# Re-ordering loads, weights and layer norm in a fused attention and MLP kernel

## The chip, the cores and the metric

The kernel runs on one core of one Trainium2 chip. TensorE (PE, with its weight loads as PEld), VectorE (DVE), ScalarE (ACT), GpSimd (POOL) and SyncE (SP, which here only issues DMAs) each work through their own queue in order. The metric is the device time of one execution in microseconds; lower is better.

## The reference

Causal attention with a position bias for 8 batches of 8 heads, 576 tokens and 64 dimensions, then a layer norm and a two-layer MLP on the heads put side by side, with a residual.

```python
scores = (1 / sqrt(64)) * q @ k.T
cum = cumsum(maximum(s, 0), axis=-1)
bias = -(cum[:, :, :, None] - cum[:, :, None, :])
scores = where(causal, -1e9, scores + minimum(bias, 0))
attn = softmax(scores)                      # 8 x 8 x 576 x 576
x = heads side by side of (attn @ v)        # 8 x 576 x 512
xn = (x - mean(x)) / sqrt(var(x) + 1e-6) * g_ln
out = x + maximum(xn @ w_ch1, 0) @ w_ch2    # 512 -> 2048 -> 512
```

## The kernel before

The order is written out by hand. The main loop has 64 **slots**, n = 0 to 63, one for each head h of each batch b. The 576 tokens are four blocks of 128 and a rest of 64.

A slot does, in this order: `scores(b, h)` (five matmuls into three PSUM tiles sa, sb, sc; one exponential on ACT for each; four triangular masks on POOL); in even slots `scores_d`, the 64 x 64 rest blocks of two heads (tile sd); two units of MLP work; `pv` of the head before (15 matmuls into the single tile pot, and then on DVE a reciprocal and two scaled copies, called the evacuation below); two more units. The softmax sum comes out of a column of ones in v.

The scores need q and k with the head dimension on partitions (qT, kT), with four more rows that carry the bias as bf16 parts of the cumulative sum; `aug` writes these by small DMAs. Each qT or kT buffer holds four heads, and there are two of each. `qk_pair` makes the 64 main rows for two heads: 10 TensorE transposes into two PSUM tiles (tag tr), four DVE copies out of them. It stands in even slots, at their start, for the two heads that begin two slots later. The tag tr has two buffers, which trqk (qk_pair), sd (scores_d) and trx (layer norm) share.

Loads for the next batch go out on SP's queue, two tiles of 256 KB in a slot, and POOL turns them to bf16 one slot later. q, k and v all lie in DRAM as (head, token, 64), and each tile takes 128 tokens of 8 heads, so that every piece is one token of one head, 256 bytes. q is scaled by 1/8 in its cast.

**Weights.** In the eight slots of batch 0, `w1_part` and `w2_part` load and cast two parts of the weights at the start of each slot: 16 parts of 512 KB through two staging buffers. The w1 cast, with the layer-norm gain folded in, is DVE's, and the w2 cast POOL's.

**Layer norm.** `ln_stats` takes statistics in two parts, after pv of heads 5 and 7; `ln_aggr` adds them up, with a power on POOL for the inverse root. At the end of slot h = 1 of the next batch `ln_tile` follows for all four tiles of the batch (five in odd batches, where the fifth, xm, holds the 64-token rests of two batches): xn on DVE, four transposes on PE, a copy on DVE, tile by tile.

**MLP units.** Then 32 units are queued: 16 `mlp1` (four matmuls into a ph tile and a relu, every fourth on DVE and the others on ACT) and 16 `mlp2` (a quarter of a py tile each; after the last quarter DVE adds the residual and SP sends the rows). ph and py share two buffers. Four units run in a slot, so the units of batch 0 begin in slot 10. After slot 63 follow the last units of batch 6, the layer norm of batch 7, and 64 units: batch 7 and the rest rows of all batches.

Of the kernel before, what the change touches and what calls it, by code (L numbers as in the profile page):

```python
# [12 lines left out]
ALU = mybir.AluOpType  # L13
# [6 lines left out]
def kernel(  # L20
# [33 lines left out]
    xnp = ctx.enter_context(tc.tile_pool(name="xnp", bufs=3))  # L54
# [16 lines left out]
    q_bf = [const.tile([P, NT, H, D], BF16, name=f"q_bf{i}") for i in range(2)]  # L71
    k_bf = [const.tile([P, NT, H, D], BF16, name=f"k_bf{i}") for i in range(2)]
# [17 lines left out]
    nc.sync.dma_start(out=c_in, in_=s_flat)  # L90


    def load(src, b, t, h0, h1, eng):
        pn = P if t < NF else TL
        tmp = stage.tile([P, h1 - h0, D], F32, name="qkvtmp", tag="st")
        eng.dma_start(
            out=tmp[:pn],
            in_=src[b, h0:h1, t * P : t * P + pn, :].rearrange("h s d -> s h d"),
        )
        return tmp, pn  # L100

    def cast(kind, b, t, h0, h1, tmp, pn, eng):
        if kind == "v":
            dst = v_bf[b % 2][:pn, t, h0:h1, 0:D]
        else:
            dst = (q_bf if kind == "q" else k_bf)[b % 2][:pn, t, h0:h1, :]
        if eng == "act":
            nc.scalar.activation(
                out=dst, in_=tmp[:pn], func=ACT.Copy, scale=scale if kind == "q" else 1.0
            )  # L110
        elif eng == "dve":
            if kind == "q":
                nc.vector.tensor_scalar_mul(out=dst, in0=tmp[:pn], scalar1=scale)
# [12 lines left out]

    first = [(n, t, 0, 4) for t in range(NT) for n in ("k", "q")]
    first_tmp = []
    for i, (n, t, h0, h1) in enumerate(first[:6]):
        first_tmp.append(load(SRC[n], 0, t, h0, h1, nc.sync))  # L130

    make_identity(nc, ident)
    nc.vector.memset(c_one, 1.0)
    nc.vector.memset(mhalf, -0.5)
    for i in range(2):
        nc.gpsimd.memset(q_bf[i][TL:P, NF, :, :], 0.0)
        nc.gpsimd.memset(k_bf[i][TL:P, NF, :, :], 0.0)
# [16 lines left out]
    nc.vector.tensor_copy(out=c_mid, in_=c_in)
    nc.vector.tensor_tensor(out=c_in, in0=c_in, in1=c_mid, op=ALU.subtract)
    nc.vector.tensor_copy(out=c_lo, in_=c_in)

    def aug(b, g):
        r0 = b * H + g * G
        i = (b * 2 + g) % 2  # L160
        for j, src in ((1, c_hi), (2, c_mid), (3, c_lo)):
            nc.sync.dma_start(out=kT[i][D + j : D + j + 1, :, 0:S], in_=src[r0 : r0 + G, :])
        nc.sync.dma_start(out=qT[i][D : D + 1, :, 0:S], in_=c_neg[r0 : r0 + G, :])


    def qk_pair(b, j):
        g, i = j // 2, (b * 2 + j // 2) % 2
        hh = (j % 2) * 2
        for src, dst in ((k_bf, kT), (q_bf, qT)):
            tr = ps_t.tile([P, SP], BF16, name="trqk", tag="tr")  # L170
# [353 lines left out]
```

## Time and profile before

| | us |
|---|---|
| median of 3 runs | 502.89 |
| the runs | 500.87 to 503.55 |
| the profiled execution, its own time | 504.88 |
| its span, first to last instruction | 503.2 |
| TensorE busy | 397.9 (79%) |
| DVE, ACT, POOL busy | 245.9, 174.1, 174.9 |

Shares over the whole span mix a stretch that waits for loads (up to about 94 us), one in which attention and MLP are interleaved (94 to 442 us), and a tail of MLP units alone. The page's 40 slices and its chain of waits tell these apart.

### The profile page before, as it was taken

The page shows a single profiled execution, that of the slowest core. Times are in us where ns is not written, and L with a number is a line of the kernel's source. Part 1 is how long each engine was busy: PE and PEld are TensorE (multiplying, and loading weights), DVE is VectorE, ACT ScalarE, POOL GpSimd, SP SyncE. Part 2 cuts the span into 40 slices and gives each one's busy share as a digit, 9 for nine tenths or more (in the row PEclk, how much of TensorE's full clock was granted, in tenths as well). Part 3 has the DMA queues.
Part 4 walks back from the last instruction along what each step waited for, and adds up shares of the span by engine and source line. Part 5 has one row for each costly group of instructions (what it writes and reads, how often), then busy time and mean ns, then how long its engine had stood idle before and what let it go on. Part 6 is the DMA issues. An engine that isn't in the chain of part 4 may idle for free.

```text
span 503.2 us, 8135 instructions
## 1 busy us (share of the span) xinstructions
PE 397.9 (79%) x2960; PEld 212.6 (42%) x2960; DVE 245.9 (49%) x614; ACT 174.1 (35%) x343; POOL 174.9 (35%) x439
## 2 busy tenths in 40 slices
PE   0303655899779987998699969986999799699996
PEld 0102434455345544554355535543554455344442
DVE  8324545447644554466445554665455445612111
ACT  2022422373226422642165226422642264041220
POOL 9324487253514442444334424442343122000000
PEclk9998555699959995999599979997999799999999
DMA  5499899141554056406640574066401000100103
GB/s 101 103 219 271 228 280 221 18 86 32 150 104 87 24 136 126 86 7 150 129 85 3 149 136 86 11 150 126 86 21 57 22 1 22 42 21 30 55 8 76
DMA packets 122487, 47.10 MB, mean 94 GB/s; under 512 B 114448, under 2 KB 114704, under 8 KB 122448
## 3 DMA queue, kind: packets, MB, share of 16 engines
q1 hardware_dynamic: 122448, 46.60, 40.4%
q8 instruction: 23, 0.38, 0.3%
q14 instruction: 16, 0.13, 0.1%
HBM read 36.85 MB, written 9.44 MB: 92 GB/s over the span
## 4 chain that ended last, share of the span: by engine, by line
PE 69%; DVE 14%; DMA 8%; POOL 5%; issue 1%; SPq 1%; POOLq 0%
PE ph L339 27%; PE py L357 25%; PE pot L260 5%; DMA w1tmp<-in_moe_w_ch_dram 4%; PE trx L329 4%; DVE xn L319 3%; DMA w2tmp<-in_moe_w_ch_dram 3%; DVE xT L334 2%; DVE kT L178 2%; PE sb L189 2%; PE sc L189 2%; PE sa L189 2%; DVE yo L366 2%; DVE hT L347 2%; PE trqk L172 2%; DVE kT L177 2%
## 5 line engine op out<-in xcount | busy, mean ns | idle before, releaser
L357 PE MATMUL py<-w_bf,hT 128*128 128x512 bf16 x576 | 135.2, 383 | 0.0
L209 POOL TENSOR_SCALAR_AFFINE_SELECT e<-e 128x128 bf16<-128x128 bf16 x256 | 71.7, 295 | 169.1 <-ACT e L199 150.6
L339 PE MATMUL ph<-xT,w_bf 128*128 128x512 bf16 x512 | 129.3, 400 | 0.0
L199 ACT ACTIVATE e<-sa 128x512 bf16<-128x512 f32 x64 | 38.2, 597 | 189.8 <-PE sa L189 183.2
L349 ACT ACTIVATE hT<-ph 128x512 bf16<-128x512 f32 x108 | 64.8, 600 | 80.4 <-PE ph L339 79.8
L339 PEld LDWEIGHTS <-w_bf 128*128 128x128 bf16 x576 | 55.2, 101 | 62.4 <-issue 13.3
L357 PEld LDWEIGHTS <-hT 128*128 128x128 bf16 x576 | 53.6, 98 | 56.8 <-issue 1.6
L268 DVE RECIPROCAL rinv<-pot 128x5 f32<-128x5 f32 x64 | 12.5, 195 | 110.5 <-PE pot L260 110.4
L260 PEld LDWEIGHTS <-e 128*128 128x128 bf16 x960 | 41.5, 103 | 23.4 <-POOL e L209 8.3
L260 PE MATMUL pot<-v_bf,e 128*128 128x65 bf16 x960 | 44.5, 202 | 7.0 <-POOL e L209 7.0
L329 PE MATMUL trx<-ident,xn 128*128 128x128 bf16 x144 | 18.5, 269 | 37.8 <-DVE xn L319 37.8
L347 DVE TENSOR_SCALAR hT<-ph 128x512 bf16<-128x512 f32 x36 | 24.9, 692 | 46.0 <-PE ph L339 46.0
L189 PEld LDWEIGHTS <-kT 68*128 68x128 bf16 x320 | 28.8, 109 | 25.1 <-issue 8.5
L207 ACT ACTIVATE e<-sc 128x512 bf16<-128x512 f32 x64 | 38.7, 605 | 0.0
L203 ACT ACTIVATE e<-sb 128x512 bf16<-128x512 f32 x64 | 37.9, 592 | 0.0
L225 PE MATMUL sd<-qT,kT 68*128 68x64 bf16 x64 | 8.3, 216 | 35.8 <-DVE kT L178 35.8
L366 DVE TENSOR_TENSOR yo<-py,xb 128x512 f32<-128x512 f32 x32 | 22.1, 690 | 25.8 <-PE py L357 25.3
L172 PE MATMUL trqk<-ident,k_bf 128*128 128x128 bf16 x160 | 18.5, 256 | 18.9 <-POOL k_bf L123 14.1
L329 PEld LDWEIGHTS <-xn 128*128 128x128 bf16 x144 | 10.5, 115 | 47.1 <-DVE xn L319 46.9
L123 POOL CAST v_bf<-qkvtmp 128x512 bf16<-128x512 f32 (+3 forms) x39 | 22.1, 587 | 23.9 <-DMA qkvtmp<-in_v_dram 23.9
L189 PE MATMUL sc<-qT,kT 68*128 68x320 bf16 (+1 forms) x128 | 28.6, 311 | 0.0
L189 PE MATMUL sb<-qT,kT 68*128 68x64 bf16 (+1 forms) x128 | 28.6, 308 | 0.0
(60 smaller groups left out, 391.2 us busy)
## 6 DMA issues: line engine op xcount, KB each, us to landing
out_dram<-yo SPq DMA_DIRECT2D x32, 256.0 KB
qkvtmp<-in_k_dram SPq DMA_DIRECT2D x28, 256.0 KB
qkvtmp<-in_q_dram SPq DMA_DIRECT2D x28, 256.0 KB
qkvtmp<-in_v_dram SPq DMA_DIRECT2D x28, 256.0 KB
w1tmp<-in_moe_w_ch_dram SPq DMA_DIRECT2D x8, 512.0 KB
w2tmp<-in_moe_w_ch_dram SPq DMA_DIRECT2D x8, 512.0 KB
qkvtmp<-in_k_dram SPq DMA_DIRECT2D x15, 128.0 KB
qkvtmp<-in_q_dram SPq DMA_DIRECT2D x15, 128.0 KB
```

Of the source, the lines that this page charges most:

```text
L189: nc.tensor.matmul(dst, lhsT=kk[0:KA, hh, kb * P : (kb + 1) * P], rhs=qq[0:KA, hh, q0:q1], start=True, stop=True,)
L199: nc.scalar.activation(out=e[:, u, 0:512], in_=a, func=ACT.Exp)
L203: nc.scalar.activation(out=e[:, u, OB : OB + 512], in_=a, func=ACT.Exp)
L207: nc.scalar.activation(out=e[:, u, OC : OC + 512], in_=a, func=ACT.Exp)
L209: nc.gpsimd.affine_select(out=e[:, u, o : o + P], in_=e[:, u, o : o + P], compare_op=ALU.is_ge, fill=0.0, base=0, pattern=[[1, P]], channe ...
L260: nc.tensor.matmul(pot[:, t, :], lhsT=e[:, u, o : o + P], rhs=vv[:, kb, h, :], start=(kb == 0), stop=(kb == last),)
L329: nc.tensor.transpose(tr[:, kd, :], xn[:, kd * P : (kd + 1) * P], ident)
L339: nc.tensor.matmul(ph, lhsT=w1_bf[:, kd, fb * P : (fb + 1) * P], rhs=xT[:, kd, :], start=(kd == 0), stop=(kd == KD - 1),)
L347: nc.vector.tensor_scalar_max(out=hT[:, fb, :], in0=ph, scalar1=0.0)
L349: nc.scalar.activation(out=hT[:, fb, :], in_=ph, func=ACT.Relu)
L357: nc.tensor.matmul(py[0], lhsT=hT[:, fb, t * P : (t + 1) * P], rhs=w2_bf[:, fb, :], start=(fb == 0), stop=(fb == FB - 1),)
L366: nc.vector.tensor_add(out=yo, in0=py[0], in1=x)
```

## The change

- **q and k loads.** One load brings two heads of one batch: 96 partitions, six neighbouring tokens on each, so that a piece is 6 x 64 floats, 1,536 bytes. `qk_pair` then has 12 transposes of 96 columns, one for each of the six tokens, and its four copies read the PSUM tile with a step of 96 elements to put the tokens back in order. It stands in odd slots, for the two heads that begin in the next slot. v is loaded as before.
- **Scale.** The factor 1/8 moves from the q cast into the exponential; the cumulative sums are multiplied by 8.
- **Order of loads and casts.** A function `pre(n)` lists them by slot; from slot 17 on it casts one q or k tile in a slot and loads the one two pairs ahead. In batch 0 and 1 some casts go to DVE and ACT.
- **Weights.** w1 is loaded in slots 2 and 9, w2 from slot 10, through four buffers; the casts stand in slots 9 to 14.
- **Start.** The first loads are heads 0 to 3 of q and k; the first two `aug` go through ACT's queue; fills of qT, kT and v_bf change size and engine.
- **Layer norm.** `ln_xn` does all xn tiles of a batch right after its statistics (slot h = 0); `ln_tr` does transposes and copies in slots h = 1 (two tiles) and h = 2 (the others), with an MLP unit between. The units of a batch are queued after slot h = 2; those of batch 0 still begin in slot 10, with three in slots 14 to 17.
- **relu.** DVE takes the first MLP unit of each slot if it is an mlp1, instead of every fourth.

The core of the diff (`cast` and `ld` take care of names and buffers):

```diff
-    stage = ctx.enter_context(tc.tile_pool(name="stage", bufs=8))
-    wst = ctx.enter_context(tc.tile_pool(name="wst", bufs=2))
+    stage = ctx.enter_context(tc.tile_pool(name="stage", bufs=2))
+    pairs = ctx.enter_context(tc.tile_pool(name="pairs", bufs=3))
+    wst = ctx.enter_context(tc.tile_pool(name="wst", bufs=4))
...
+        nc.sync.dma_start(
+            out=tmp[0:QP],
+            in_=src[b, 2 * j : 2 * j + 2].rearrange("h (p t) d -> p h (t d)", t=QT),
+        )
...
-            for t in range(NT):
+            for t in range(QT):
                 nc.tensor.transpose(
-                    tr[:, t * P : (t + 1) * P],
-                    src[b % 2][:, t, 2 * j : 2 * j + 2, :],
-                    ident,
+                    tr[:, t * QP : (t + 1) * QP],
+                    src[0:QP, t, :, :],
+                    ident[0:QP, 0:QP],
                 )
-            nc.vector.tensor_copy(out=dst[i][0:D, hh, :], in_=tr[0:D, :])
-            nc.vector.tensor_copy(out=dst[i][0:D, hh + 1, :], in_=tr[D : 2 * D, :])
+            for u in range(2):
+                copy_on(
+                    engs[n],
+                    dst[i][0:D, hh + u, 0:S].rearrange("d (p t) -> d p t", t=QT),
+                    tr[u * D : (u + 1) * D, :].rearrange("d (t p) -> d p t", t=QT),
+                )
...
+        elif n == 9:
+            cast("v", 1, 4, "pool")
+            for i in range(4):
+                cast_w1(i)
+                ld_w1(4 + i)
...
-        if h == 1 and b > 0:
-            for t in range(len(x_tiles(b - 1))):
-                ln_tile(b - 1, t)
+        lt = {1: (0, 1), 2: (2, 3, 4)}.get(h, ()) if b > 1 else ()
+        if n == 9:
+            lt = range(NF)
+        for t in lt:
+            ln_tr(b - 1, t)
+            if n != 9 and t != 1 and t != 4:
+                run_units(1)
+                nu -= 1
+        run_units(nu - 2)
+        if n == 9 or (b > 1 and h == 2):
             queue += batch_units(b - 1)
```

**The layer norm on DVE.** Batch 2's, around slots h = 0 and 1 of batch 3. Before, xn and the copy xT alternate at the end of h = 1:

```order
L366 TENSOR_TENSOR yo_2135<-py_2097,xb_818 128x512
L319 TENSOR_SCALAR xn_2139<-xb_1454,mv_2057,rs_2058 128x512
L334 COPY xT_2138<-trx_2141 128x4x128
L319 TENSOR_SCALAR xn_2147<-xb_1454,mv_2057,rs_2058 128x512
L334 COPY xT_2138<-trx_2149 128x4x128
```

Now:

```order
L348 TENSOR_SCALAR xn_2017<-xb_1424,mv_2004,rs_2005 128x512
L404 TENSOR_TENSOR yo_2029<-py_1962,xb_754 128x512
L108 COPY kT0_106<-trqk_2038 64x576 x2
L108 COPY qT0_104<-trqk_2047 64x576 x2
L297 RECIPROCAL rinv_2097<-pot_2081 128x5
L299 TENSOR_TENSOR xb_2080<-pot_2081,rinv_2097 128x4x64
L306 TENSOR_SCALAR xm1_112<-pot_2081,rinv_2097 64x64
L369 COPY xT_2012<-trx_2101 128x4x128
L369 COPY xT_2012<-trx_2111 128x4x128
```

All xn now stand together in h = 0, ahead of qk_pair's copies; the copies xT stand behind those and behind an evacuation.

**An mlp1 slot with a qk_pair on DVE.** Before, the fourth relu of the slot ahead stands in front of the copies:

```order
L347 TENSOR_SCALAR hT_96<-ph_2316 128x512
L177 COPY kT1_108<-trqk_2328 64x640
L178 COPY kT1_108<-trqk_2328 64x640
L177 COPY qT1_106<-trqk_2336 64x640
L178 COPY qT1_106<-trqk_2336 64x640
L268 RECIPROCAL rinv_2392<-pot_2376 128x5
```

Now:

```order
L108 COPY kT1_107<-trqk_2209 64x576 x2
L108 COPY qT1_105<-trqk_2218 64x576 x2
L385 TENSOR_SCALAR hT_99<-ph_2242 128x512
L297 RECIPROCAL rinv_2270<-pot_2254 128x5
L299 TENSOR_TENSOR xb_2080<-pot_2254,rinv_2270 128x4x64
```

The relu of the slot's own first unit now follows the four copies.

**SP's queue in batch 0.** Before, weights stand between the loads of q and k from the first slot on:

```order
L413 DMA gln<-in_moe_g_ln_dram 128x4x1
L420 DMA w1tmp<-in_moe_w_ch_dram 128x1024 x2
L96 DMA qkvtmp<-in_k_dram 128x8x64
L96 DMA qkvtmp<-in_q_dram 128x8x64
L420 DMA w1tmp<-in_moe_w_ch_dram 128x1024 x2
```

Now:

```order
L90 DMA ktmp<-in_k_dram 96x2x384
L90 DMA qtmp<-in_q_dram 96x2x384
L491 DMA gln<-in_moe_g_ln_dram 128x4x1
L90 DMA ktmp<-in_k_dram 96x2x384
L90 DMA qtmp<-in_q_dram 96x2x384
L99 DMA vtmp<-in_v_dram 128x8x64 x3
L90 DMA ktmp<-in_k_dram 96x2x384
L90 DMA qtmp<-in_q_dram 96x2x384
L145 DMA w1tmp<-in_moe_w_ch_dram 128x2x512 x4
```

Half of w1 is issued in batch 0, behind nearly half of batch 1's loads, and the rest from slot 9.

## Rows read from the trace of the kernel before

**Rows 1.** The page: the span in 40 slices of 12.6 us.

```profile
PE   0303655899779987998699969986999799699996
PEclk9998555699959995999599979997999799999999
DMA  5499899141554056406640574066401000100103
GB/s 101 103 219 271 228 280 221 18 86 32 150 104 87 24 136 126 86 7 150 129 85 3 149 136 86 11 150 126 86 21 57 22 1 22 42 21 30 55 8 76
```

**Rows 2.** Start, in order of time: start, duration, engine, operation [idle before, releaser].

```profile
4.30 0.42 ACT L108 ACTIVATE k_bf<-qkvtmp 128x256 bf16<-128x256 f32 x1 [2.24 <-DMA qkvtmp<-in_k_dram]
8.11 0.42 ACT L108 ACTIVATE k_bf<-qkvtmp 128x256 bf16<-128x256 f32 x1 [1.39 <-DMA qkvtmp<-in_k_dram]
8.40 2.22 POOL L141 MEMSET qT<- 4x2560 bf16 x1
8.68 2.25 DVE L154 CAST c_mid<-c_in 64x576 bf16<-64x576 f32 x1
19.37 0.63 PE L189 MATMUL sa<-qT,kT 68*128 68x512 bf16 x1
36.65 0.75 DVE L421 TENSOR_SCALAR w_bf<-w1tmp,gln 128x1024 bf16<-128x1024 f32 x1 [0.71 <-DMA w1tmp<-in_moe_w_ch_dram]
38.48 0.29 PE L225 MATMUL sd<-qT,kT 68*128 68x64 bf16 x2 [17.61 <-DVE kT L178]
```

**Rows 3.** The chain that ended last, its landmarks: start, duration, engine and line.

```profile
94.21 3.41 PE ph L339 x8
...
397.79 3.41 PE ph L339 x8
...
428.11 5.18 PE py L357 x24
...
442.39 14.30 PE ph L339 x64
456.68 13.81 PE py L357 x64
...
498.64 0.69 DVE yo L366
```

**Rows 4.** The same chain over two slots between layer norms.

```profile
206.72 0.69 DVE hT L347
...
208.36 0.23 PE sd L225 x2
208.59 1.73 PE ph L339 x8
210.32 0.46 PE pot L260 x15
...
212.51 0.22 PE sa L189
...
217.10 0.69 DVE hT L347
```

**Rows 5.** Groups by shape: count | busy us, mean ns | idle before, releasers.

```profile
L178 DVE COPY kT<-trqk 64x640 bf16<-64x640 bf16 x32 | 15.8, 493 | 0.4
L270 DVE TENSOR_TENSOR xb<-pot,rinv 128x256 f32<-128x256 f32 x64 | 27.2, 425 | 2.2
L366 DVE TENSOR_TENSOR yo<-py,xb 128x512 f32<-128x512 f32 x32 | 22.1, 690 | 25.8 <-PE py L357 25.3 <-issue 0.3
L334 DVE COPY xT<-trx 128x512 bf16<-128x512 bf16 x32 | 13.6, 425 | 19.5 <-PE trx L329 19.5
L306 POOL TENSOR_TENSOR rs<-rs,mhalf 128x5 f32<-128x5 f32 x4 | 4.7, 1176 | 16.2 <-DVE rs L305 16.2
```

**Rows 6.** Layer norm of one batch on DVE, in order of time.

```profile
231.59 0.20 DVE L268 RECIPROCAL rinv<-pot 128x5 f32<-128x5 f32 x1 [1.50 <-PE pot L260]
232.60 0.87 DVE L295 BATCH_NORM_STATS2 stats<-xb 128x6 f32<-128x128 f32 x4
234.10 0.17 DVE L305 TENSOR_SCALAR rs<-mv 128x5 f32<-128x5 f32 x1
238.49 0.54 DVE L319 TENSOR_SCALAR xn<-xb,mv,rs 128x512 bf16<-128x512 f32 x1
```

**Rows 7.** Busy time by stretch: PE, PEld, DVE, ACT, POOL, then granted clock, DMA.

```profile
190.00:196.40 6.40, 4.42 (x30) 3.05 (x31) 4.14 (x9) 0.87 (x2) 0.20 (x1) 0.50 1.19 203
196.40:199.80 3.40, 3.40 (x12) 1.22 (x11) 0.00 (x0) 1.45 (x4) 2.31 (x7) 0.50 0.01 2
206.70:217.10 10.40, 9.94 (x88) 5.41 (x86) 5.06 (x12) 6.77 (x13) 4.77 (x13) 1.00 0.54 101
```

More of the change, by code (lines that the diff above doesn't have):

```diff
@@ L102, in cast, with copy_on @@
-    def cast(kind, b, t, h0, h1, tmp, pn, eng):
+        tmp = stage.tile([P, H, D], F32, name="vtmp", tag="vtmp", bufs=3)
+        nc.sync.dma_start(
+            out=tmp[:pn], in_=v[b, :, t * P : t * P + pn, :].rearrange("h s d -> s h d")
+        )
+        return tmp
+    def copy_on(eng, out, in_):
+        if eng == "act":
+            nc.scalar.copy(out=out, in_=in_)
+        elif eng == "dve":
+            nc.vector.tensor_copy(out=out, in_=in_)
+        else:
+            nc.gpsimd.tensor_copy(out=out, in_=in_)
@@ L154, with cast @@
[L154 to L158, printed above, removed]
+            loaded[kind, b, i] = load_qk(k if kind == "k" else q, b, i, kind + "tmp")
+    def cast(kind, b, i, eng):
+        if b >= B:
+            return
+        tmp = loaded.pop((kind, b, i))
+        if kind == "v":
+            pn = P if i < NF else TL
+            copy_on(eng, v_bf[b % 2][:pn, i, :, 0:D], tmp[:pn])
+        else:
+            t = pairs.tile([P, QT, 2, D], BF16, name=kind + "p", tag=kind + "p")
+            copy_on(
+                eng,
+                t[0:QP].rearrange("p t h d -> p h t d"),
+                tmp[0:QP].rearrange("p h (t d) -> p h t d", d=D),
+            )
+            ready[kind, b, i] = t
@@ L425, in w2_part, with run_units @@
-    def w2_part(c):
-        tmp = wst.tile([P, 2, Dm], F32, name="w2tmp", tag="w")
-        nc.sync.dma_start(out=tmp, in_=w2_r[:, 2 * c : 2 * c + 2, :])
-        nc.gpsimd.tensor_copy(out=w2_bf[:, 2 * c : 2 * c + 2, :], in_=tmp)
     queue = []
     pend = []
-    def run_units(n):
-        for _ in range(n):
+    def run_units(n, dve_first=False):
+        for i in range(n):
             if queue:
+                first_unit[0] = dve_first and i == 0
                 queue.pop(0)()
-    slots = [(b, h) for b in range(B) for h in range(H)]
@@ new lines @@
+    c_in, c_sc, c_one = c_in[0:BH], c_sc[0:BH], c_one[0:BH]
+    nc.sync.dma_start(out=c_in, in_=s.rearrange("b h s -> (b h) s"))
+    ld("k", 0, 0)
+    ld("q", 0, 0)
+    ld("k", 0, 1)
+    ld("q", 0, 1)
+    for t in range(3):
+        ld("v", 0, t)
+    make_identity(nc, ident)
+    nc.vector.memset(c_one, 1.0)
+    nc.vector.memset(ones4, 1.0)
+    for i in range(2):
+        nc.vector.memset(kT[i][0:KA, :, S:SP], 0.0)
+        nc.scalar.dma_start(out=kT[i][D + 3 : D + 4, :, 0:S], in_=ones4)
@@ new lines @@
+    nc.vector.tensor_copy(out=c_mid, in_=c_in)
+    nc.vector.tensor_tensor(out=c_lo, in0=c_in, in1=c_mid, op=ALU.subtract)
+    cast("k", 0, 1, "act")
+    qk_pair(0, 0, ("act", "act", "dve", "dve"))
+    aug(0, 0, nc.scalar)
+    nc.vector.memset(qT[1][D : D + 3, :, :], 1.0)
+    aug(0, 1, nc.scalar)
+    for i in range(2):
+        nc.gpsimd.memset(v_bf[i][:, 0:NF, :, D : D + 1], 1.0)
+        nc.gpsimd.memset(v_bf[i][TL:P, NF, :, :], 0.0)
+        nc.gpsimd.memset(v_bf[i][0:TL, NF, :, D : D + 1], 1.0)
@@ L462 @@
+    NU = {10: 4, 11: 4, 12: 4, 13: 4, 14: 3, 15: 3, 16: 3, 17: 3, 18: 4}
+    for n in range(B * H):
+        b, h = n // H, n % H
+        nu = NU.get(n, 4)
+        pre(n)
+        if h % 2 == 1 and n > 1:
+            g = (n + 1) // 2
+            qk_pair(g // 4, g % 4)
         scores(b, h)
+        if n == 0:
+            qk_pair(0, 1)
+        run_units(1, True)
         if h % 2 == 0:
             scores_d(b, h // 2)
-        run_units(2)
+        run_units(1)
         if pend:
@@ L494 @@
     queue += mixed_units()
-    run_units(len(queue))
+    while queue:
+        run_units(4, True)
 _INS = ['q', 'k', 'v', 's', 'moe_g_ln', 'moe_w_ch1', 'moe_w_ch2']
```

337 lines of the change are left out of this document (199 added, 138 removed).

## The prediction

> **What bounds the kernel now.** I read the 40 slices first, then the chain that ended last, then each stage by its own rows. The slices show three stages [rows 1]. In the first seven, to about 90 us, PE is busy 0 to 6 tenths while DMA moves over 200 GB/s in five of them. From then to slice 35 PE stands at 9 tenths, with a dip once a batch in which the granted clock drops too. The last five are MLP alone.
>
> *Start and batch 0.* The first scores run at 19.37 us and the second slot's only behind the scores_d at 38.48, after PE idled 17.6 us [rows 2]. It waited for DVE's copies into kT, and DVE for a w1 load: the cast at 36.65 stands ahead of the copies in DVE's queue. Weights gate all eight slots like this, and the first MLP unit starts at 94.21 [rows 3].
>
> *Main stage.* Six batches take 397.79 - 94.21 = 303.6 us, 50.6 each [rows 3]. Two slots between layer norms take 217.10 - 206.72 = 10.4 us [rows 4] with PE busy 9.94 at full clock [rows 7], so PE is the bound there: eight such slots would be 41.5. [...]
>
> *Tail.* From 428.11 on, six units, a layer norm, two units, and 64 units in 56 us, PE-bound [rows 3].
>
> **The change part by part.** The prices of PE work come from rows 4: a unit is 1.73 / 2 = 0.87 us; scores 3 x 0.22 = 0.65; pv 0.46; scores_d 0.12, half of its 0.23, since the next unit overlaps its tail. For the new transposes (12 of 96 columns for 10 of 128) I take 0.55 as an estimate: all of an even slot, 212.51 - 206.72 = 5.8, less the wait of the scores_d, leaves about that.
>
> *The new copies* decide most. Today 64x640 costs 0.493 and 128x512 bf16 0.425 [rows 5], 0.53 ns an element over a base of 0.155, so 576 would cost 0.46. From PSUM in float32, 256 cost 0.425 and 512 cost 0.690: 1.04 ns an element. Both are 4 bytes in 1.04 ns, and the bf16 rows get two neighbours for it. The new copies read with a step of 96 elements, so 4 bytes hold one wanted element: 0.16 + 576 x 1.04 ns = 0.76 us. I take 0.76 with 0.46 as the lower end; no row reads bf16 with a step, so the upper end is open, and the third rival prices it.
>
> [...]
>
> *Start.* The s load and four q/k loads go out first; before, six tiles of 128 KB land between the casts at 4.30 and 8.11 [rows 2], 0.2 MB a us, so the first 2.1 MB (to the third v tile) land by 12. DVE gets one more fill (2560 elements; POOL's took 2.22) ahead of the cumulative sum, whose casts take up to 2.25 each [rows 2], and has c_lo by 12. The aug DMAs follow on ACT and land at 15: first scores at 15, where 19.4 stands now. The last v tile is issued only when DVE has cast an earlier one, behind two copies and another 2.2 us fill: at 16, landing at 18.5; DVE then casts k and copies, and the second slot's scores run at 21 (now 38.6).
>
> *Slots 1 to 7.* No weight cast stands in them. DVE has, per two slots, four copies (3.04), two evacuations of 1.0 (231.59 to 232.60 [rows 6]) and a cast of some 0.6: 5.6 us, and statistics once. PE at half clock needs about as much. Since the chain copies, scores, pv, evacuation closes on itself I take 3.45 a slot: slot 8 at 45.3.
>
> *Slots 8 and 9* load DVE most. After pv at 47.6: evacuation 1.0, statistics and sums 1.5 (1.67 for five tiles, 232.60 to 234.27 [rows 6]), the power on POOL 1.1 [rows 5], four xn of 0.5 to 0.54 [rows 6], eight half-size w1 casts of 0.45 (0.75 for twice the size [rows 2]), four copies, an evacuation, four xT copies of 0.425 with their transposes. That is 63; with the scores of slot 10 at half clock the **first MLP unit starts at 64** instead of 94.2.
>
> *Weights.* What is left of w1 and w2 then, 6.3 MB, moves behind slots 9 to 14 with 0.6 MB of q and k, from 54 us to the unit that needs the last part, near 90. At the 219 to 280 GB/s of the weight slices [rows 1] that is 25 to 32 us of 36: hidden. The w2 casts, about 1 us each, fall on POOL between masks that pv needs a slot later; they too are covered.
>
> *Main slots.* An even slot is 0.65 + 0.12 + 0.46 + 4 x 0.87 = 4.7: the scores_d finds its PSUM buffer free, since the copies now end a slot earlier. An odd one is 0.55 + 0.65 + 0.46 + 3.46 = 5.1. In mlp1 slots the relu of the first unit stands behind the four copies: copies from 0.45 to 3.55 after the slot's start, relu to 4.3. The third unit wants that PSUM buffer, and PE gets to it at 3.4: it waits 0.9, twice a batch.
>
> *Layer norm.* Count from the start of slot h = 0. pv ends at 2.95; DVE then needs 1.0 + 1.67, POOL's power 1.18, five xn 2.5, a yo 0.69 [rows 5, 6], and is at 10.0. Then come the four copies of slot h = 1, and the first transposes of the layer norm need the PSUM buffer of the k copies: 11.5. PE gets there at 4.7 + 3.4 = 8.1 and waits 3.4, and 0.4 for the next. The idle can drop the clock again; as the echo cost 1.7 (half of 3.4 [rows 7]) when it came, I take 1.0.
>
> A batch: 4 x 4.7 + 2 x 5.1 + 2 x 6.0 + 4.5 x 0.22 for transposes (four of 128 columns stream what sa's 512 do) + 3.8 + 1.0 = **46.9**, against 50.6.
>
> *Sum.* First unit at 64. To the start of slot 19: 32 units 27.7, eight scores 5.2, nine pv 4.1, transposes and scores_d 3.9, mlp1 waits 1.8, a layer norm with two units fewer to cover it 5.6, cold start 1.7: 50, so 114. Five batches of 46.9: 348.5. Slots 59 to 63: 26, so 374.5. Tail: pv, 76 units 65.8, transposes 1.1, 0.5 twice for relus (14.30 against 13.81 [rows 3]), 1.5 for the layer norm among seven units: 69.9, so 444.4. Last add and store as now, 503.2 - 498.64 = 4.6: a span of 449.0. The profiled execution took 1.7 more than its span, and the median lies 2.0 below it: **449**.
>
> **The rivals.**
>
> *1. The copies keep today's rate (0.46).* Then the mlp1 waits go (14 x 0.9 = 12.6), each of six layer norms waits 1.0 less (6), and batches 0 and 1 lose some 6 of DVE work: 424. For it: today's copies are all at that rate. Against it: the 4 bytes a step above.
>
> *2. Loads hold the start after all, so that the change doesn't do what it says there.* Up to slot 10, 7.1 MB of q, k, v and 2.1 MB of w1 must come, at 165 GB/s if slot 9 is to be where I put it. Rows 1 show 101 and 103 GB/s in the first two slices, where SP's queue waited on casts, and the new order also waits for casts on three engines. At 130 GB/s the first unit would be 14 us later: 463; and should weights also come late in slots 10 to 14, up to 475. Against it: 1,536-byte pieces, and 219 to 280 GB/s once the queue is full.
>
> *3. Strided copies cost far more, and DVE is the bound: slower than before.* Without them DVE has per batch 8 evacuations, statistics, five xn and xT, four relus and four yo, 21.9 us; with 16 copies at 0.76 it is 34, below 46.9. Each 0.1 us on a copy adds 1.6. To lose all 54 us in six and a half batches, a batch must take 55: copies of 2.1 us, from where it decides. At 2.3 the batch is 58.7 and the time 526. For it: no row shows the pattern. Against it: float32 from PSUM with a step (out of pot, 65 apart) costs its plain 1.04 ns an element.
>
> **How the numbers follow.** Forecast 449 (437 to 461 by the slot rate of batch 0 and the clock after layer norms): 0.62. Rival 1, 418 to 432: 0.16. Rival 2, 455 to 478: 0.18. Rival 3, above 503: 0.03; near no change, if two of them meet: 0.01. The range 424 to 470 takes in the middle of rival 1 and most of rival 2. A measurement of this kernel can tell about 0.5% from no change; faster by more 0.96, within 0.01, slower by more 0.03.
>
> **What would show it.** Copies of 0.76 (or 0.46) in the groups by shape. First MLP unit near 64, with DVE and not DMA ahead of it in the chain. PE waits of some 0.9 for the relu's buffer in odd mlp1 slots, and of 3 to 4 in slot h = 1, with a smaller clock dip. 47 us from batch to batch. Batch 0 slots that wait for loads, or a batch of over 50 us, would prove the sum wrong.

## The result, and the profile after

The changed kernel takes 446.46 us (median of 4 runs, 445.89 to 447.1) beside 502.19 for the kernel before on the same chip: a ratio of 0.889, with a 95% interval of 0.886 to 0.892. The prediction was 449, with 424 to 470 as its range. The profiled execution took 447.1 with a span of 445.4. One of e6's four runs below fell into a slower state (448.2 us, at a granted clock of 0.928 where the others had 0.943 to 0.959) and is left out of its median.

The page of after, the 40 slices of 11.1 us, to be held against [rows 1]:

```profile
PE   1396459995999799969998899889997999999995
...
PEclk9999999997999899988999999969999999999999
DMA  7887075964531354134511551154221000101013
GB/s 198 214 231 199 10 243 174 271 197 119 143 107 55 101 149 115 29 96 129 142 56 52 162 152 54 53 149 125 71 76 47 26 1 24 72 0 72 24 26 71
```

PE stands at 9 tenths from the seventh slice on (67 us), with dips; before, from the ninth (101 us). The first two slices move 198 and 214 GB/s where they moved 101 and 103. PE's dips in the main stage are still there, once a batch, but shallower, and so are those of the clock: from 118 us on its lowest slices are at 6 and 8 tenths, where those of before stand at 5 and 7.

The landmarks of the start, from the order of time on PE (start, duration, engine, line, operation, count, and in brackets the idle time before it with its releaser):

```profile
14.57 0.59 PE L213 MATMUL sa<-qT,kT 68*128 68x512 bf16 x1 [6.91 <-DMA qT<-c_neg]
...
21.17 0.58 PE L213 MATMUL sa<-qT,kT 68*128 68x512 bf16 x1 [1.26 <-ACT e L222]
...
43.71 0.61 PE L213 MATMUL sa<-qT,kT 68*128 68x512 bf16 x1 [2.41 <-DVE qT L108]
...
58.37 0.61 PE L364 MATMUL trx<-ident,xn 128*128 128x128 bf16 x4 [7.81 <-DVE kT L108]
...
63.45 0.63 PE L377 MATMUL ph<-xT,w_bf 128*128 128x512 bf16 x1
```

Where [rows 2] have scores at 19.37 and the second slot's not before 38.48, they now start at 14.57 and 21.17, and the first MLP unit comes at 63.45. On the same view of before it comes at 94.02, so the start gave 30.6 us. The first units of later batches follow at 117.98, 163.27, 211.23, 255.31, 303.33 and 347.41: five periods of 45.9 us on average, where before has 50.3. That gave 21.9 more, and these two make up 52.4 of the 57.8 us by which the span fell; the period from the first to the second batch is 2.2 longer, and what follows the last of these units 7.6 shorter.

The copies into kT and qT, from the groups by shape (count, then busy us, mean ns, then idle before and its releaser):

```profile
L108 DVE COPY kT<-trqk 64x576 bf16<-64x576 bf16 x62 | 46.6, 751 | 8.3 <-PE trqk L191 7.5
L108 DVE COPY qT<-trqk 64x576 bf16<-64x576 bf16 x64 | 48.3, 754 | 1.4
```

They cost half as much again as the larger copies of [rows 5], as forecast.

One layer norm of five tiles, in order of time on POOL, DVE and PE:

```profile
193.04 1.17 POOL L335 TENSOR_TENSOR rs<-rs,mhalf 128x5 f32<-128x5 f32 x1 [2.95 <-DVE rs L334]
...
194.25 2.39 DVE L348 TENSOR_SCALAR xn<-xb,mv,rs 128x512 bf16<-128x512 f32 x4 [1.29 <-POOL rs L335]
...
197.74 1.51 DVE L108 COPY kT<-trqk 64x576 bf16<-64x576 bf16 x2
199.28 1.52 DVE L108 COPY qT<-trqk 64x576 bf16<-64x576 bf16 x2
199.30 0.61 PE L364 MATMUL trx<-ident,xn 128*128 128x128 bf16 x4 [3.98 <-DVE kT L108]
```

And the busy times there, as in [rows 7]: stretch, its length, PE, PEld, DVE, ACT, POOL busy, then granted clock, DMA share and GB/s:

```profile
195.20:199.30 4.10, 0.12 (x5) 0.00 (x2) 4.02 (x9) 0.00 (x0) 2.58 (x5) 0.79 0.14 51
199.30:204.80 5.50, 5.27 (x21) 2.64 (x23) 3.74 (x8) 0.53 (x2) 0.00 (x0) 0.54 0.44 114
```

DVE works without a gap from the power on POOL to the kT copies, and PE stands still beside it for 4 us; behind that the granted clock is 0.54 for 5.5 us. The layer norm is spread, but one wait in front of it is left, and it is DVE's queue that holds it.

### The profile page after: what moved, and what is told of

It reads as the page before. It is cut to its first block, busy times and chain, and to the rows that moved or that the text cites. A ratio compares the mean times of both kernels' runs of the same rounds, so it can differ in the third digit from the quotient of the medians.

```text
span 445.4 us, 8185 instructions
## 1 busy us (share of the span) xinstructions
PE 377.6 (85%) x2973; PEld 208.6 (47%) x3024; DVE 280.8 (63%) x615; ACT 174.1 (39%) x339; POOL 171.4 (38%) x415
## 4 chain that ended last, share of the span: by engine, by line
PE 65%; DVE 17%; issue 7%; POOL 5%; ACT 3%; DMA 1%; POOLq 0%; SPq 0%; ACTq 0%
PE ph L377 27%; PE py L395 21%; PE pot L289 4%; DVE xn L348 4%; DVE kT L108 4%; PE sa L213 3%; PE sb L213 3%; PE trqk L191 3%; DVE qT L108 3%; PE sc L213 2%; PE trx L364 2%; ACT hT L387 2%; POOL rs L335 2%; DVE yo L404 1%; POOL e L236 1%
## 5 line engine op out<-in xcount | busy, mean ns | idle before, releaser
L236 POOL TENSOR_SCALAR_AFFINE_SELECT e<-e 128x128 bf16<-128x128 bf16 x256 | 77.3, 315 | 169.4 <-ACT e L222 169.1
L395 PE MATMUL py<-w_bf,hT 128*128 128x512 bf16 x550 | 140.1, 392 | 1.9 <-issue 0.7
L377 PE MATMUL ph<-xT,w_bf 128*128 128x512 bf16 x489 | 121.3, 382 | 4.9 <-ACT hT L387 3.3
L395 PEld LDWEIGHTS <-hT 128*128 128x128 bf16 x576 | 54.3, 100 | 52.4 <-issue 4.6
L108 DVE COPY kT<-trqk 64x576 bf16<-64x576 bf16 x62 | 46.6, 751 | 8.3 <-PE trqk L191 7.5
L108 DVE COPY qT<-trqk 64x576 bf16<-64x576 bf16 x64 | 48.3, 754 | 1.4
L213 PEld LDWEIGHTS <-kT 68*128 68x128 bf16 x320 | 27.2, 106 | 37.3 <-issue 17.1
L364 PE MATMUL trx<-ident,xn 128*128 128x128 bf16 x144 | 16.3, 247 | 29.3 <-DVE kT L108 26.0
L213 PE MATMUL sa<-qT,kT 68*128 68x512 bf16 x64 | 27.7, 433 | 11.5 <-DMA qT<-c_neg 6.9
L299 DVE TENSOR_TENSOR xb<-pot,rinv 128x256 f32<-128x256 f32 x64 | 27.2, 425 | 2.2
L110 POOL CAST qp<-qtmp 96x768 bf16<-96x768 f32 x31 | 26.2, 846 | 4.4 <-DMA qtmp<-in_q_dram 4.4
```

The lines of the kernel that those rows point to most:

```text
L108: nc.vector.tensor_copy(out=out, in_=in_)
L110: nc.gpsimd.tensor_copy(out=out, in_=in_)
L213: nc.tensor.matmul(dst, lhsT=kk[0:KA, hh, kb * P : (kb + 1) * P], rhs=qq[0:KA, hh, q0:q1], start=True, stop=True,)
L236: nc.gpsimd.affine_select(out=e[:, u, o : o + P], in_=e[:, u, o : o + P], compare_op=ALU.is_ge, fill=0.0, base=0, pattern=[[1, P]], channe ...
L299: nc.vector.tensor_tensor(out=xb[b][:, :, hs], in0=pot[:, 0:NF, 0:D], in1=rinv[:, 0:NF].unsqueeze(2).to_broadcast([P, NF, D]), op=ALU.mult,)
L364: nc.tensor.transpose(tr[:, kd, :], xn[:, kd * P : (kd + 1) * P], ident)
```

## The experiments

My theory had four parts: the weights had held the start; the copies cost 0.75 us because of their step of 96 elements; DVE is on the path only in batches 0 and 1 and at the layer norm; what is left of the layer norm is DVE's order. The rivals: copies on the path everywhere, large load pieces as the source of the gain, and a spread layer norm that merely moved the wait.

The first units in the table are read from the order of time on PE; "per batch" is the mean of the five periods behind the second batch's first unit. In the kernel before, e4 and e5 a batch's units start in slot h = 2, in e6, e10, e11 and e13 in h = 4, in the others in h = 3, so columns two and three compare only within such a group; the periods compare everywhere. The ratios are to the kernel before, measured on the same chip beside it.

| kernel | first unit | second batch | per batch | median us | ratio (95%) |
|---|---|---|---|---|---|
| before | 94.0 | 146.3 | 50.3 | 502.9 | 1 |
| after | 63.5 | 118.0 | 45.9 | 446.5 | 0.889 (0.886 to 0.892) |
| e3, weights in batch 0 | 93.3 | 147.0 | 45.6 | 477.3 | 0.951 (0.946 to 0.957) |
| e4, before with weights late | 74.6 | 134.5 | 50.4 | 492.2 | 0.980 (0.976 to 0.983) |
| e5, layer norm serial | 65.4 | 120.5 | 49.2 | 469.0 | 0.929 (0.923 to 0.934) |
| e8, plain copies, 1,536 B | 58.4 | 111.6 | 44.3 | 431.5 | 0.857 (0.852 to 0.861) |
| e1, plain copies, 256 B | 58.7 | 115.5 | 43.9 | 433.9 | 0.859 (0.855 to 0.864) |
| e14, v of batch 2 earlier | 63.7 | 118.5 | 45.8 | 445.5 | 0.888 (0.885 to 0.891) |
| e6, layer norm a slot later | 63.3 | 119.2 | 45.0 | 442.3 | 0.878 (0.873 to 0.883) |
| e10, and xn behind the copies | 63.3 | 116.0 | 41.2 | 421.0 | 0.839 (0.835 to 0.843) |
| e11, e10 and e1 together | 59.0 | 109.7 | 40.2 | 408.2 | 0.813 (0.811 to 0.816) |
| e13, e11 and e14 together | 58.8 | 111.2 | 40.2 | 409.9 | 0.816 (0.813 to 0.819) |

### The weights: e3 and e4

e3 is after with the loads and casts of the weights in batch 0 again:

```diff
+        if b == 0:
+            for i in (2 * h, 2 * h + 1):
+                if i < 8:
+                    ld_w1(i)
+                    cast_w1(i)
+                else:
+                    ld_w2(i - 8)
+                    cast_w2(i - 8)
         pre(n)
```

(and the ld_w and cast_w lines of pre taken out).

> After the change, but the weights are loaded and cast as before it: two parts at the start of each slot of batch 0 (w1 casts on DVE, w2 casts on POOL); everything else is as after. My theory (the start was held by weights that stood ahead of the copies in DVE's and ahead of q, k and v in SP's queue): the second slot's scores come at 30 or later instead of 21, the first MLP unit at 85 to 95 instead of 64, slots 10 to 17 get 2 to 5 us back since no cast stands in them: 465 to 475. Rival (large load pieces and copies that need no v or weights ahead are what made the start short; the weights fit in beside them): first unit by 70, 446 to 452.

Measured 477.3 us, 31 more than after, with the first unit at 93.27: within the forecast of 85 to 95, and 2 us above the range of the time. The second slot's scores come at 27.2, later than the 21.2 of after but not at 30 or later. Two rows on DVE and PE, in order of time:

```profile
49.48 0.88 DVE L155 TENSOR_SCALAR w_bf<-w1tmp,gln 128x512 bf16<-128x512 f32 x2 [6.67 <-DMA w1tmp<-in_moe_w_ch_dram]
...
53.91 0.61 PE L213 MATMUL sa<-qT,kT 68*128 68x512 bf16 x1 [9.97 <-DVE qT L108]
```

DVE waits 6.7 us for a w1 load, two casts and the copies follow, and PE has waited 10 us. That is the pattern of [rows 2] again in the changed kernel, and the rival (weights fit in beside larger loads) is out. One more part of my expectation missed: the slots after the first unit got next to nothing back. The next batch's first unit comes 53.7 us later with no weight cast there, and 54.5 us later in after, so the casts in slots 10 to 14 are indeed covered. Those of slot 9 are not: there e3's PE waits 4.64 us before the layer norm's first transposes, and 7.81 in after, where eight w1 casts stand ahead of the copies on DVE.

```profile
88.20 0.61 PE L364 MATMUL trx<-ident,xn 128*128 128x128 bf16 x4 [4.64 <-DVE kT L108]
```

e4 is the other direction: the kernel before, its weights moved to slots 2 and 9 to 14, all else left.

```diff
-        if b == 0:
-            for i in (2 * h, 2 * h + 1):
...
+        if n == 2:
+            ld_w1(0), ld_w1(1), ld_w1(2)
+        elif n == 9:
+            for i in range(3):
+                cast_w1(i)
+                ld_w1(3 + i)
+        elif n == 10:
+            cast_w1(3), ld_w1(6)
...
+        elif n == 14:
+            cast_w2(4), ld_w2(7)
+            for i in range(5, 8):
+                cast_w2(i)
```

> The kernel before, with this part of the change alone: the weights are loaded and cast in slots 2 and 9 to 14 (three buffers for them, taken from the staging of q, k and v and from the outputs). Copies, load pieces and layer norm are those of before. My theory: the first unit comes at 66 to 75 instead of 94, some of it is given back in slots 10 to 17, 475 to 483. Rival A (the pieces of 256 bytes would hold the start now that the weights are gone): first unit at 80 or later, 488 to 496. Rival B (parts of the change only work together): 500 to 503.

Measured 492.2, only 9.6 us less than before, though the first unit comes 19.5 us earlier. My figure of 475 to 483 was wrong, and neither rival describes it: the first unit's time agrees with mine, the total with rival A's. Two things are in the trace. First, without any weights the second slot's scores still start only at 33:

```profile
13.45 0.57 SPq L162 DMA_DIRECT2D kT<-c_lo  x1
...
14.75 0.68 SPq L96 DMA_DIRECT2D qkvtmp<-in_q_dram  x1
...
31.48 0.30 DVE L115 CAST v_bf<-qkvtmp 128x256 bf16<-128x256 f32 x1 [1.61 <-DMA qkvtmp<-in_v_dram]
31.80 0.48 DVE L177 COPY kT<-trqk 64x640 bf16<-64x640 bf16 x1
...
32.85 0.29 PE L225 MATMUL sd<-qT,kT 68*128 68x64 bf16 x2 [11.79 <-DVE kT L178]
```

These are SP's DMA issues, then two rows of DVE and one of PE. From 7.5 to 14.7 us SP issues no load: the rows of c_hi, c_mid, c_lo and c_neg stand there, which need the sums, and every q, k and v load behind them goes out later. DVE waits for one such load after the other, the last for 1.61 us, and the copies into kT follow. In after these rows go out on ACT's queue. So of the 17.3 us from 38.48 to 21.17 by which the second slot moved forward, some 5.6 (38.48 to 32.85) came with the weights alone; no run here divides the rest between the order of the loads and the other changes to the start. Second, 7.7 us are given back in the next batch (60.0 from first unit to first unit, 52.3 before), where PE waits for the w2 casts:

```profile
102.50 0.59 PE L357 MATMUL py<-w_bf,hT 128*128 128x512 bf16 x2 [1.35 <-POOL w_bf L439]
106.22 1.01 PE L357 MATMUL py<-w_bf,hT 128*128 128x512 bf16 x2 [3.12 <-POOL w_bf L439]
```

Moving the weights alone, with three buffers for them where after has four, is thus worth 10 us, and taking that part back out of the whole costs 31: what a part is worth depends on the others.

### The copies and the load pieces: e8 and e1

Both read PSUM without the step. e8 keeps the 1,536-byte pieces:

```diff
-                    dst[i][0:D, hh + u, 0:S].rearrange("d (p t) -> d p t", t=QT),
-                    tr[u * D : (u + 1) * D, :].rearrange("d (t p) -> d p t", t=QT),
+                    dst[i][0:D, hh + u, 0:S],
+                    tr[u * D : (u + 1) * D, :],
```

> After the change with its large load pieces, but the copies into kT and qT read PSUM in its own order, so the columns of kT and qT stay in the order of the transposes: putting the tokens in order is the part of the computation that is left out. The instructions and their sizes are otherwise the same. My theory: copies 0.46 instead of 0.75, and 5 to 15 us less in all (431 to 441), the same as the kernel with 256-byte pieces within 2 us, since there the loads are ahead of use. Rival A (copies on the path everywhere): 424 or less. Rival B (pieces decide at the start): this one is 5 us or more faster than the kernel with 256-byte pieces. Rival C (the step costs nothing, 0.75 is the price of this tile): copies stay at 0.75 and the time at 446.

e1 has the same lines, and puts token 96 t + p in partition p, so that a load is made of 256-byte pieces and the order is right without a step:

```diff
-            out=tmp[0:QP],
-            in_=src[b, 2 * j : 2 * j + 2].rearrange("h (p t) d -> p h (t d)", t=QT),
+            out=tmp[0:QP].rearrange("p h (t d) -> p (h t) d", d=D),
+            in_=src[b, 2 * j : 2 * j + 2].rearrange("h (t p) d -> p (h t) d", t=QT),
```

> After the change, but with 96 partitions holding tokens 96 apart, so that the copies into kT and qT read their PSUM tile without a step; each q/k load is then made of 256-byte pieces again. Both parts at once: copies and piece size. My theory (the step of 96 elements is what makes a copy cost 0.75 us; DVE is on the path only in batches 0 and 1 and at the layer norm; large pieces matter little because DMA is ahead of its use): copies at about 0.46, the first MLP unit 2 to 5 us earlier than 64, one layer-norm wait about 1 us shorter, so 5 to 15 us less in all: 431 to 441. Rival A (copies are on the path everywhere, as the first rival of the prediction priced them): 424 or less. Rival B (the large pieces are what fed the start): slots 0 to 9 wait for loads, the first unit comes at 68 or later, and the time is 450 or more.

Measured 431.5 and 433.9, 15 and 13 us less than after, both within 431 to 441, as my theory had it. The copies of e8, by shape, and its layer norm on PE:

```profile
L108 DVE COPY kT<-trqk 64x576 bf16<-64x576 bf16 x62 | 28.0, 451 | 8.8 <-PE trqk L191 8.1
```

```profile
190.19 0.61 PE L364 MATMUL trx<-ident,xn 128*128 128x128 bf16 x4 [3.38 <-DVE kT L108]
```

The same 576 elements cost 0.451 us without the step and 0.751 with it, so rival C is out. The first unit comes 5.0 us earlier, and each later batch is 1.6 shorter (44.3 against 45.9), of which the layer norm's wait accounts for 0.6 (3.98 to 3.38) and the waits for a relu's buffer, which are gone, for 0.5. Rival A (424 or less) is out: the copies are not on the path everywhere. The two differ by 2.4 us, a little over the 2 I allowed and less than the 5 that rival B asked for, and their intervals overlap: whether the larger pieces bring anything at all stays open, and it is no more than that. The first two slices of e1 move 208 and 163 GB/s with 256-byte pieces, so the 101 and 103 of before were not the pieces' doing either.

### The layer norm: e5, e6 and e10

e5 runs xn, transposes and copy tile by tile at the end of slot h = 1, as before the change:

```diff
-        lt = {1: (0, 1), 2: (2, 3, 4)}.get(h, ()) if b > 1 else ()
...
+        if h == 1 and b > 0:
+            for t in range(len(x_tiles(b - 1))):
+                ln_xn1(b - 1, t)
+                ln_tr(b - 1, t)
+            queue += batch_units(b - 1)
```

> After the change, but with the layer norm as before it: at the end of slot h = 1, xn, four transposes and a copy run tile by tile, one after the other, in front of the batch's units; nothing is spread over slots, and all slots run four units. My theory: PE waits 5 to 7 us in each of six layer norms instead of 4 and the clock falls for as long behind it: 3 to 5 us more a batch in six batches, 465 to 476. Rival A (spreading brought nothing, since the wait moved to the first transposes of slot h = 1 and the clock falls there all the same): 444 to 450. Rival B (the spread norm is what makes the batch 45.9 instead of 50.6, so all of that gain comes back): 474 to 478.

Measured 469.0, 22.5 us more than after and 3.3 a batch: my theory. PE waits before each of the five transposes,

```profile
211.57 0.40 PE L379 MATMUL trx<-ident,xn 128*128 128x128 bf16 x4 [1.80 <-DVE xn L363]
...
212.95 0.40 PE L379 MATMUL trx<-ident,xn 128*128 128x128 bf16 x4 [0.97 <-DVE xn L363]
```

0.97 each after the first, so 5.7 us where after waits 4.0 and 0.6. With this the spread norm is worth 3.3 of the 4.4 us by which a batch fell; where the remaining 1.1 comes from, no run here takes apart.

e6 keeps the spread but puts the transposes one slot later:

```diff
-        lt = {1: (0, 1), 2: (2, 3, 4)}.get(h, ()) if b > 1 else ()
+        lt = {2: (0, 1), 3: (2, 3, 4)}.get(h, ()) if b > 1 else ()
...
-        if n == 9 or (b > 1 and h == 2):
+        if n == 9 or (b > 1 and h == 3):
```

> After the change, but the transposes of the layer norm come one slot later (two tiles in slot h = 2, the rest in h = 3) and the batch's units are queued a slot later; slots 14 to 19 run some units fewer so that units are left to fill slot h = 2. My theory (PE waits 4 us a layer norm because DVE reaches the xn of the first tiles only then, and the clock falls after that idle time): the wait goes, the granted clock stays at 1.00, the batch falls from 45.9 to 41 to 43: 420 to 432. Rival A (DVE is late by as much wherever the transposes stand, since xn and copies stand in one queue): 440 to 450. Rival B (the clock falls for another reason than this idle time): the wait goes but the clock still falls, 430 to 438.

Measured 442.3, 4 us less than after, where I had expected 420 to 432. My theory fell and rival A stands: the wait moved.

```profile
196.37 1.54 DVE L108 COPY qT<-trqk 64x576 bf16<-64x576 bf16 x2
...
197.18 0.39 PE L213 MATMUL sa<-qT,kT 68*128 68x512 bf16 x1 [3.06 <-DVE qT L108]
```

Now it is the scores of slot h = 2 that wait, for the qT copies of slot h = 1, which stand behind five xn and POOL's power in DVE's queue. So it is not the transposes' place but DVE's order. e10 adds that:

```diff
                 ln_aggr(pb)
-                ln_xn(pb)
+                if pb == 0:
+                    ln_xn(pb)
         pend.append((b, h))
+        if h == 1 and b > 1:
+            ln_xn(b - 1)
```

> The layer norm one slot later as in the run before it, and xn for batches from the second on is issued at the end of slot h = 1, behind that slot's copies into kT and qT on DVE, instead of ahead of them. Copies have their step of 96. With the later transposes alone PE's wait moved from the transposes to the first scores of slot h = 2, for the copies into qT, 1.8 to 3.1 us a batch. My theory (it is DVE's order, five xn and POOL's power ahead of the copies, that PE waits for): no wait over 0.5 us in slots h = 1 to 3, the clock stays at 1.00, the batch falls from 45.0 to 42 to 43 and the time to 424 to 432. Rival A (DVE is full there, and something else comes late by as much, the transposes or the first unit's relu): 438 to 444. Rival B (the wait goes but the clock falls all the same): 432 to 438.

Measured 421.0, 25 us less than after, my theory, and 3 below its range. The same place in order of time:

```profile
185.41 1.54 DVE L108 COPY qT<-trqk 64x576 bf16<-64x576 bf16 x2
...
187.14 0.38 PE L213 MATMUL sa<-qT,kT 68*128 68x512 bf16 x1
...
187.74 1.89 DVE L348 TENSOR_SCALAR xn<-xb,mv,rs 128x512 bf16<-128x512 f32 x4
...
190.04 0.39 PE L364 MATMUL trx<-ident,xn 128*128 128x128 bf16 x4
```

Neither the scores nor the transposes wait, and POOL's power is done before DVE comes to the xn. The main stage of after, of e10, and of e11 below, each as one stretch (columns as above):

```profile
118.00:347.40 229.40, 207.00 (x1778) 116.47 (x1809) 157.71 (x355) 100.97 (x201) 103.86 (x249) 0.96 0.35 97
```

```profile
116.00:322.00 206.00, 201.35 (x1810) 113.69 (x1808) 154.92 (x355) 100.47 (x201) 101.69 (x248) 1.00 0.37 104
```

```profile
109.70:310.50 200.80, 199.77 (x1810) 113.39 (x1808) 132.11 (x355) 100.51 (x201) 99.52 (x248) 1.00 0.44 108
```

PE's idle time in it falls from 22.4 us to 4.7, and the granted clock goes from 0.96 to 1.00: without the wait there is no dip behind it.

### Both together: e11, and the v tiles: e14 and e13

e11 is e10 with the lines of e1.

> The kernel with xn behind the copies and the layer norm a slot later, and also 256-byte load pieces with copies that read PSUM without a step: the two ideas together. My theory (both shorten the same wait at the layer norm, so they don't add up there; what the copies save in batches 0 and 1, 5 to 6 us, is on top): 417 to 425, 5 to 8 below the kernel with the step. Rival (they add up in full, 13 us): 411 to 417.

Measured 408.2, 12.8 us below e10: the rival's sum, and lower even than its range. By the table 4.3 us of it come before the first unit, 2.0 in the period behind it and 5.2 in the five that follow. I had taken the batch's share of e1's gain for the layer norm's wait alone. The last two stretches above show what it is: once PE no longer waits there, it has still 4.7 us of small waits in e10's main stage, among them two of 0.96 where a unit wants the buffer of a relu that stands behind four copies in DVE's queue, and in e11 1.0 us in all; it is also busy 1.6 us less there. With PE busy for 199.8 of 200.8 us at full clock, what is left of that stage is PE's own work.

e14 is after with two v tiles of batch 2 loaded and cast earlier, since PE waits for them in slot 17:

```diff
-            ld("v", 2, 2)
+            ld("v", 2, 2), ld("v", 2, 3)
...
-            ld("v", 2, 3), ld("v", 2, 4)
+            ld("v", 2, 4)
+            cast("v", 2, 3, "pool")
         elif n > 16:
+            if n == 17:
+                cast("v", 2, 4, "pool")
...
-            if n == 17:
-                cast("v", 2, 3, "pool")
-                cast("v", 2, 4, "pool")
```

> After the change, but in slots 15 to 17 the v tiles of batch 2 are loaded and cast one step earlier: tile 3 a slot earlier, tile 4 first thing in slot 17. In the profile of after, PE waits 1.6 and 0.9 us for these casts in slot 17, and 2.1 us more for the layer norm's first transposes. My theory (the layer norm on DVE sets that slot, since the kernel with the weights in batch 0 waits 1.5 us for v and 4.7 us there, 6 to 7 us of idle PE in all against 4.6): the wait for v goes, the wait for the layer norm grows by as much, 445 to 447. Rival (the late casts of v are the path): 441 to 444.

Measured 445.5, ratio 0.888 against 0.889: no difference, as expected. Slot 17 on PE in after, and the transposes' wait in e14:

```profile
103.22 0.31 PE L289 MATMUL pot<-v_bf,e 128*128 128x65 bf16 x5 [1.64 <-POOL v_bf L110]
104.42 0.19 PE L289 MATMUL pot<-v_bf,e 128*128 128x65 bf16 x1 [0.89 <-POOL v_bf L110]
106.69 0.61 PE L364 MATMUL trx<-ident,xn 128*128 128x128 bf16 x4 [2.08 <-DVE kT L108]
```

```profile
107.81 0.61 PE L364 MATMUL trx<-ident,xn 128*128 128x128 bf16 x4 [5.22 <-DVE kT L108]
```

The wait for v only hid the wait for DVE: 1.64 + 0.89 + 2.08 are 4.6 us, and with the v tiles there in time 0.5 (for the last of them) + 5.2 remain.

e13 is e11 with the same lines.

> The fastest kernel so far (xn behind the copies, layer norm a slot later, 256-byte pieces and copies without a step) with the same earlier v tiles in slots 15 to 17. There PE waits 1.5 us for the v casts and for nothing else in that slot. My theory (with the layer norm's wait gone the wait for v is on the path): the wait goes, 405.5 to 407.5. Rival (something else is late by as much there): 407.5 to 409.

Measured 409.9, not faster than e11 (408.2): my expectation of 405.5 to 407.5 fell, although DVE's old wait is gone there. Again another took its place:

```profile
106.07 0.42 PE L191 MATMUL trqk<-ident,kp 96*128 96x96 bf16 x6 [2.11 <-DVE xT L369]
```

The xn of that layer norm, two of them beside POOL's casts of q, k and v, take 3.15 us for four and 1.60 for the fifth there (2.38 and 0.53 in e11); they delay the copy into xT, and with it the PSUM buffer that the next q and k transposes need. What a v tile earlier brings is lost there.

## Why the prediction was right, point by point

**The sum.** Held against the trace, its terms stand so. First unit 63.5 for 64. From there to slot 19, where the first transposes are at 116.0: 52.6 for 50. Five batches: 229.4 for 234.5. Slots 59 to 63, to the last pv at 370.8: 25.3 for 26. From there to the last add at 440.66: 69.9 for 69.9. Add and store 4.7 for 4.6. The errors are -0.5, +2.6, -5.1, -0.7, 0 and +0.1: the span is 445.4 for 449.0. It was right to 0.8%, and part of that is luck: terms that were too high and too low offset each other, as follows. Without the excess of the relu's term below (9.3 us over the run) it would have stood at 439.7, 1.3% too low.

**Copies: right.** 0.751 and 0.754 for 0.76. That price was an estimate from the rates of [rows 5], 4 bytes in 1.04 ns; the runs have 0.75 with the step and 0.45 without it (e8), and how DVE comes to that price no run here shows.

**Start: right in its times, only half right in its reason.** 14.6, 21.2 and 43.7 for 15, 21 and 45.3 (the start of slot 8). The prediction put the 17.6 us of idle time before the second slot on a w1 load. e4 shows that without it the slot still comes at 33, since DVE then waits for loads of q, k and v that go out late in SP's queue. The sum placed every load of the new order, but the reason does not name this. For slots 2 to 7 e3 confirms the reason. Within slot 8 the xn were mis-sized: 3.95 us for four, where the sum took 0.5 to 0.54 each; slot 8's start, 1.6 us early, made up for it.

**Weights hidden: right for slots 10 to 14.** There e3 gains 0.8 us from not having the casts. The eight w1 casts of slot 9 are on the path, where the sum had placed them, at 8 x 0.45 us; e3's wait there is 3.2 us shorter. The stretch to slot 19 took 2.6 us more than the sum, but not for its waits: PE's 4.6 us in slot 17, which e14 shows to be the layer norm's, are below the 5.6 priced for it, and the relu's waits are shorter too. What has no term there is the clock behind that wait. From 106.7 to 112.3 us it is granted 0.50, which makes PE's 5.4 us of work there some 2.7 longer by this estimate, half of them (four matmuls of a unit take 1.89 us at 110.51, at 0.50, and 1.03 at 112.30, at 1.00).

**Main slots: right.** The sum's batch without any waits is 40.2: its terms add up to 46.8 (the prediction has 46.9, a slip of 0.1), less 3.8, 1.0 and 1.8. e11, whose main stage has almost no waits, has a batch of 40.2.

**The wait for the relu's buffer: wrong.** The sum has 0.9 twice a batch, since the third unit should want the buffer of the first one, whose relu stands behind the copies on DVE. One odd slot of after:

```profile
164.98 0.60 ACT L387 ACTIVATE hT<-ph 128x512 bf16<-128x512 f32 x1 [0.53 <-PE ph L377]
...
165.63 1.91 PE L377 MATMUL ph<-xT,w_bf 128*128 128x512 bf16 x8 [0.23 <-ACT hT L387]
165.77 0.69 DVE L385 TENSOR_SCALAR hT<-ph 128x512 bf16<-128x512 f32 x1
```

The third unit starts before DVE has even begun the first one's relu: it takes the buffer of the second, which ACT has released. It waits 0.23, and over the run 3.3 us in 14 waits instead of 12.6. (In e10 a unit does wait for DVE's relu, 0.96, but only twice in the five main batches.) This is the term that made the forecast too high. It also counts in the first rival's 424, whose 25 us held these 12.6, of which 3.3 were there to be gained: with the copies at 0.45, e8 measured 431.5.

**Layer norm: right in its place and its size.** PE waits 3.98 in batches of five tiles and 2.7 in batches of four, then 0.6 and 0.3 for a buffer: 3.6 on average, for 3.8. The clock's share (the prediction's echo, the 3.4 us at 0.50 in [rows 7]), for which the sum has 1.0, can be read off the stretches above: for the same work in five batches PE is busy 207.0 us in after and 201.35 in e10 at full clock, 1.1 a batch. That size is in part luck, since the dip has another shape than the one it was taken from: behind the longest waits it lasts 5.5 us at 0.54, where [rows 7] show 3.4 at 0.50, and behind the wait of 2.71 us at 246.2 there is none (1.00).

**Rivals.** The second (loads hold the start) is out: the first unit comes at 63.45, 198 and 214 GB/s move in the first slices, and behind the first scores no wait of PE ends with a DMA; DVE still waits 2.5 us for a v tile ahead of the second slot, about where the sum has it. The third (copies of 2.1 us or more) is out by the copies' own row.

## What to carry to other kernels

When a wait is spread or moved, ask what stands in front of the awaited work in its engine's queue: the transposes' place was worth 4 us, and issuing xn behind the copies, with the same work, 21 more (the new order without the later transposes was not run). A part's worth measured alone and measured by taking it out can differ threefold (10 and 31 us for the weights): alone, it left the late loads of q, k and v in place, and PE waited for the w2 casts instead. The version to keep is e11: plain copies with 256-byte pieces, transposes in slots 2 and 3, xn behind the copies: 408.2 us, 0.813 of the kernel before.

## What the runs showed of the hardware

**The same idle time does not always cost the clock.** Two layer norms of e6 with the same wait of PE of 3.06 us, then two of after with waits of 2.72 and 2.71 (stretches behind the wait; the granted clock is the third number from the end):

```profile
197.20:203.00 5.80, 5.75 (x58) 3.54 (x60) 4.20 (x11) 1.72 (x4) 2.72 (x7) 1.00 0.69 195
...
285.00:291.00 6.00, 5.99 (x34) 3.17 (x35) 2.29 (x6) 1.85 (x4) 2.75 (x7) 0.50 0.78 209
```

```profile
152.90:158.00 5.10, 5.06 (x24) 2.47 (x25) 3.87 (x8) 0.72 (x2) 0.05 (x1) 0.67 0.50 125
...
246.20:251.00 4.80, 4.45 (x29) 2.29 (x31) 3.83 (x8) 1.69 (x4) 0.63 (x3) 1.00 0.51 128
```

At one place 1.00, at the other 0.50; 0.67 and 1.00. After the longest waits of the main stage, 3.98 us, it fell both times, to 0.54. What decides between them no run here shows.

**An xn beside casts on POOL took 1.60 us, beside affine_selects 0.53.** In e5, where POOL stands idle meanwhile, an xn takes 0.54 us. In slot 8 of after, four of them take 3.95:

```profile
49.77 3.95 DVE L348 TENSOR_SCALAR xn<-xb,mv,rs 128x512 bf16<-128x512 f32 x4 [1.15 <-POOL rs L335]
```

A pair that does the same work differs in what POOL does beside it, the fifth xn of the same layer norm in e13 and in e11:

```profile
102.75 1.60 DVE L348 TENSOR_SCALAR xn<-xm,mv,rs 128x512 bf16<-128x512 f32 x1
103.19 0.82 POOL L110 CAST qp<-qtmp 96x768 bf16<-96x768 f32 x1
103.95 0.86 POOL L110 CAST v_bf<-vtmp 128x512 bf16<-128x512 f32 x1
```

```profile
101.09 1.95 POOL L236 TENSOR_SCALAR_AFFINE_SELECT e<-e 128x128 bf16<-128x128 bf16 x4 [0.31 <-ACT e L222]
...
102.35 0.53 DVE L348 TENSOR_SCALAR xn<-xm,mv,rs 128x512 bf16<-128x512 f32 x1
```

Beside two casts it takes 1.60 us, beside affine_selects its plain 0.53; there it is the selects that are longer, 1.95 us for four, where four with no xn beside them take 1.04 in e5. The four in slot 8 of after are of both kinds: the last of them, with two casts beside it, takes 2.31 of the 3.95. What makes an xn longer beside casts and the selects longer beside an xn, no run here shows.
